# A three-stage kernel on one core: the halves of z take the way through device memory, four transfers home instead of sixteen

## The chip, the core and the metric

The kernel runs on one core of a Trainium2 chip. A core has five engines that run side by side, each through its own instruction stream in program order: TensorE (PE, matmuls; PEld is its weight load), VectorE (DVE), ScalarE (ACT), GpSimd (POOL), and SyncE (SP), which issues the transfers (DMAs) here. Matmuls write to PSUM, everything else works in SBUF; the inputs and the output are in device memory. An engine waits for another by semaphores.

The metric is the time of one execution on the device in microseconds (us). Before the change it is 1769.05 us, the median of 3 runs (1768.02 to 1769.48).

## The reference

Three stages, all in float32. First, attention in two steps through 32 packed tokens per head; then a mixture of 8 experts, each a two-layer network whose result is scaled by a balanced gate P; last, a two-layer network with a squared relu.

```python
p_packed = sm_attn(p, k, v)               # 4 batches, 8 heads, 576 tokens, 64 wide
out = sm_attn(q, p_packed, p_packed)
x = ...                                   # out as [2304, 512]
for e in range(8):                        # P: 8 rounds of row and column scaling
    h = np.maximum(x @ w1[e], 0.0)        # 512 -> 1024
    ye = h @ w2[e]                        # 1024 -> 512
    out += P[:, e:e + 1] * ye
h = x @ w_in                              # 512 -> 2048
g = s * (np.maximum(h, 0.0) ** 2) + b
return g @ w_out
```

## The kernel before

Every float32 operand of a large matmul is split in a high and a low part, and a product is three passes: high x high, high x low, low x high (PASSES). Tokens are kept transposed: xa holds the attention result as weights over the packed tokens of each batch, not x itself. So for the experts x @ w1 becomes two products: z = packed tokens @ w1, a small one, and then the attention weights times z. z is what the change is about.

The work of the experts is cut into 32 **units** u, 4 to an expert, each 256 columns of w1. Units 4 to 31 run in the function slotw, one call for each of the 4 batches, here called **blocks 0 to 3** of a unit. A block has five **places** n = 0 to 4. At each place stand, in this order: one of the four jobs j1 to j4 of mm1w (the first layer for this batch, matmuls of L524 into the PSUM tiles ps_a, ps_b and ps_e, followed by ACT's relu and DVE's low part into h); one tile2 of the block before (the second layer, 6 matmuls of L593 over 128 tokens, whose sum DVE puts into acc); and the side jobs given for this place. The four jobs use a form of matrix product with seven products for eight, hence the copies snap (L540) and sums (L487). Blocks 1 and 3 have four tile2 to run, blocks 0 and 2 have five. Within this stretch the order of each engine is the order written in the code (manual_schedule).

What the unit after this one needs is made by side jobs:

- w1_split (block 0): the high and low part of its w1 slice, into w1s.
- z_heads (block 2, places 0 and 2): z for one half of the heads, as 12 matmuls of L459, and two copies of ACT (L467) into a tile "stage". Partitions of stage are 32 packed tokens for each of 4 batches.
- z_home (same places): z has to lie by head group on the partitions, with the batches along the row. For each half 8 transfers of 64 KB go from stage to zp within SBUF (L476).
- z_add (L487, POOL): four sums and differences for one batch of z, from zp into sums.
- z_split (L494 and L495): for one batch, two casts on ACT give the high part zz, from zp and from sums, and two subtractions on POOL the low part. The matmuls of j1 of that batch's block read zz.

For batches 1 to 3, z_split stands at place 0 of the block before; z_add stands at place 3 two blocks before for batches 2 and 3, and at place 4 of block 3 of the unit before for batch 1. For batch 0 of the next unit z_add stands at place 1 of block 3 and z_split at place 3, after j4; the next block is block 0 of that next unit. The loads of w1 (place 2 of block 3) and of w2 (place 1 of block 0) follow z_home on SP, in the order of the code.

The tiles come from pools with few buffers: raw (2: w2 as loaded, one half of stage, and from unit 9 on also weights for the last stage), w1 (2, one of which holds the packed tokens for good), z (3: zp and two zz). A tile is written when the last reader of the one before in its buffer is through.

Of the kernel before, what the change touches and what calls it, by code (L numbers as in the profile page):

```python
# [9 lines left out]
F32 = mybir.dt.float32  # L10
# [6 lines left out]
B, H, S, HD, NPK = 4, 8, 576, 64, 32  # L17
# [3 lines left out]
NC = D // 128  # L21
FU = 256
# [21 lines left out]
def tile_kernel(ctx: ExitStack, tc: tile.TileContext, qT, kT, vv, pb, w1c, w2c, wcat64, wg, sv, bv, out):  # L44
    nc = tc.nc
    pool = lambda name, bufs=1, **k: ctx.enter_context(tc.tile_pool(name=name, bufs=bufs, **k))
    const = pool("const")
    big = pool("big")
    raw_p = pool("raw", 2)
    w_p = pool("w", 4)  # L50
    z_p = pool("z", 3)
    banks = {}

    def share(stack, **counts):
# [22 lines left out]
    def psa(tag, name):  # L77
        return banks[tag].tile([128, 512], F32, tag=tag, name=name)
# [32 lines left out]
    w1_p = []  # L111
# [12 lines left out]
    def load_w2(u, eng=G):  # L124
        r = raw_p.tile([128, 1024], F32, tag="raw", name="raw")
        nc.sync.dma_start(out=r, in_=w2c[u])
        yield
        w = w_new((2, u))
        if eng is V:
            V.tensor_copy(w[:, 0, :], r)  # L130
        else:
            A.copy(w[:, 0, :], r)
        eng.tensor_tensor(out=w[:, 1, :], in0=r, in1=w[:, 0, :].bitcast(F32), op=ALU.subtract)
# [286 lines left out]
    zq_, xt, wt_p, zplain = {}, [], [], []  # L420

    def zp_new():
        zplain[:] = [z_p.tile([128, B, 4, 128], F32, tag="z", name="zp")]
# [10 lines left out]
    pph, w1s, staged = [], {}, {}  # L434
# [16 lines left out]
    def z_heads(u, half):  # L451

        ps = [psa("y", "ps_z") for _ in range(2)]
        for j in range(2):
            c = 2 * half + j
            for n, (k, a) in enumerate(PASSES):
                for r in range(2):
                    rows = slice(64 * r, 64 * r + 64)
                    mmul(ps[r][:, j * FU:(j + 1) * FU], pph[0][rows, k, c, :], w1s[u][rows, a, c, :],  # L459
                         start=n == 0, stop=n == 2)  # L460
        if half:
            s_ = w1_p[-1].tile([128, 2, 2, FU], F32, tag="w1", name="stage1")
        else:
            s_ = raw_p.tile([128, 2, 2, FU], F32, tag="raw", name="stage0")
        staged[half] = s_
        for r in range(2):
            A.copy(s_[:, :, r, :], ps[r].rearrange("p (j m) -> p j m", j=2))  # L467

    def z_home(u, half):

        if half == 0:
            zp_new()
        for b in range(B):
            for j in range(2):
                c = 2 * half + j
                nc.sync.dma_start(out=zplain[0][32 * c:32 * c + 32, b].rearrange("k n m -> k (n m)"),  # L476
                                  in_=staged[half][32 * b:32 * b + 32, j].rearrange("k r m -> k (r m)"))

    z_sums = {}

# [211 lines left out]
    def slot1(u, pr, q, side=()):  # L692
        first = [lambda f=f: mm1a(u, pr, q, f) for f in range(UF)]
        coming.extend(made(u, pr, q))
        if u < UP:
            first.append(lambda: keep(u, q))
        slot(first, side, 0 if u < UP and (u, q) != (0, 2) else 1)

    def slotw(u, b, side):

        todo, jobs = ready[:], mm1w(u, b)
        ready[:] = made(u, b // 2, 2 * (b % 2)) + made(u, b // 2, 2 * (b % 2) + 1)
        for n in range(5):
            for q_ in (jobs, todo):
                if q_:
                    q_.pop(0)()
            for s in side.get(n, ()):
                s()
# [8 lines left out]
    def zjobs(u):  # L717

        ps = []
        t0, t1 = ("ym", "mm") if "m" in banks else ("yy", "yy")  # L720
        return [lambda: ps.extend((zmm(u, 0, tags=t0), zmm(u, 1, tags=t1))), lambda: zput(u, 0, ps[0]),
                lambda: zput(u, 1, ps[1])]
# [5 lines left out]
    def side1(u, pr, q):  # L728
        jobs = []
        if u + 1 < U1 and (pr, q) == (1, 0) and u + 1 != W0:  # L730
            jobs += zjobs(u + 1)
        if (pr, q) == (1, 1) and u + 2 < U1:
            jobs.append(lambda: load_w1(u + 2))
        if (pr, q) == (0, 1) and u + 1 < U1:
            jobs.append(lambda: list(load_w2(u + 1)))
        if u == W0 - 2 and pr == 1 and q % 2:
            jobs.append(lambda: behind_seam(x_add, q // 2))
        return jobs
# [8 lines left out]
    with tc.tile_pool(name="ppf", bufs=1) as ppf_p, tc.tile_pool(name="w1p", bufs=2) as w1_, ExitStack() as whole, ExitStack() as start:  # L747
# [3 lines left out]
        with tc.manual_schedule(), tc.tile_pool(name="at", bufs=1) as at_p, ExitStack() as early:  # L751
# [114 lines left out]
            for s in range(1, B - 1):  # L866
                n, last = s + 1, s == B - 2
# [19 lines left out]
        with tc.tile_pool(name="mid", bufs=1) as mid:  # L887
            share(start, y=3, h=2, m=3)
            bal = balance(mid)
            for u, pr, q in order[:cut]:  # L890
                side = []
                if u >= UP:
                    side = side1(u, pr, q)
                elif u == UP - 1:
                    side = zjobs(UP) if q == 2 else []
                elif q == 2:
                    side = [lambda: list(load_w2(UP))]
# [29 lines left out]
        with tc.manual_schedule():  # L927
            first = {(0, 1): [(w2_, W0), (x_split, 0)],
                     (0, 2): [(x_split, 1), (x_add, 2)],
                     (0, 3): [(w2_, W0)],  # L930
                     (1, 0): [(z_half, W0, 0), (z_half, W0, 1), (x_split, 2)],
                     (1, 1): [(x_add, 3), (load_w1, W0 + 1)],
                     (1, 2): [(z_add, W0, 0)],
                     (1, 3): [(z_split, W0, 0), (x_split, 3), (z_add, W0, 1)]}
            for u, pr, q in order[cut:]:
                slot1(u, pr, q, [lambda f=f, a=a: f(*a) for f, *a in first[pr, q]])
            for u in range(W0, U1):
                for b in range(B):
                    side, last = {n: [] for n in range(5)}, u == U1 - 1
                    if b + 1 < B:  # L940
                        side[0].append((z_split, u, b + 1))
                    if b + 2 < B:
                        side[3].append((z_add, u, b + 2))
                    if u == W0 and b == 0:
                        side[0].append((pp_split, ))
                    if last and b < 2:
                        side[2].append((split_plain, b, 0))
                        side[4].append((split_plain, b, 1))
                    if not last:
                        if b == 0:  # L950
                            side[1].append((w2_, u + 1))
                            side[2].append((w1_split, u + 1, 0))
                            side[4].append((w1_split, u + 1, 1))
                        if b == 1:
                            side[1].append((w2_, u + 1))
                        if b == 2:
                            side[0] += [(z_heads, u + 1, 0), (z_home, u + 1, 0)]
                            side[2] += [(z_heads, u + 1, 1), (z_home, u + 1, 1)]
                        if b == 3:
                            side[1].append((z_add, u + 1, 0))  # L960
                            side[3].append((z_split, u + 1, 0))
                            side[4].append((z_add, u + 1, 1))
                            if u + 2 < U1:
                                side[2].append((load_w1, u + 2))
                    if conv.get("at", 0) < steps and u > U1 // 4 or last and b:
                        side[(2, 0, 2, 1)[b]].append((more, ))
                    if last and b > 1:
                        for c in range(NC):
                            side[1 + c].append((flip, b - 2, c))
                    slotw(u, b, {n: [lambda f=f, a=a: f(*a) for f, *a in fs] for n, fs in side.items()})  # L970
        for v in range(U2):
            for b in range(NB):
                side = []
# [50 lines left out]
```

## Time and profile before

| | us |
|---|---|
| median of 3 runs | 1769.05 (1768.02 to 1769.48) |
| the profiled execution | 1768.22 |
| its span, from the first instruction to the last | 1766.4 |
| PE matmuls busy | 1703.8 (96%) |
| PE weight loads busy | 1453.1 (82%) |
| DVE busy | 1179.2 (67%) |
| POOL busy | 802.6 (45%) |
| ACT busy | 752.4 (43%) |

Units 4 to 31 fill the stretch from about 226 to 1350 us; before it stand attention, the gate and units 0 to 3, after it the last stage. The granted clock of PE was 0.999 of full speed over the span. A matmul's end is modelled in the records, and matmuls are pipelined, so the starts of groups tell more than their busy time. Busy shares of the other engines are low, but each works in order: what counts is whether a result is there when PE comes to it.

### The profile page before, as it was taken

How to read it: one execution, taken by the hardware profiler on the slowest of the kernel's cores; microseconds unless marked ns; L12 is line 12 of the kernel's file. 1: busy time of each engine (PE TensorE's matmuls, PEld its weight loads, DVE VectorE, ACT ScalarE, POOL GpSimd, SP SyncE). 2: the span in 40 equal slices, each digit the busy share in tenths (PEclk: the TensorE clock that was granted, in tenths of full speed). 3: DMA queues.
4: the chain of work that ended last, by engine and by line, in shares of the span. 5: the costliest groups of instructions: out<-in, count | busy, mean ns of one | idle time of the engine just before them, and what ended most of it. 6: DMA issues, size and time to landing. Idle time of an engine off the chain costs nothing.

```text
span 1766.4 us, 27541 instructions
## 1 busy us (share of the span) xinstructions
PE 1703.8 (96%) x10111; PEld 1453.1 (82%) x10111; DVE 1179.2 (67%) x2402; ACT 752.4 (43%) x1724; POOL 802.6 (45%) x970
## 2 busy tenths in 40 slices
PE   6999999999999999999999999999999999999999
PEld 4678877888888888788888888878888899999998
DVE  4646555566666666666666666656668888888864
ACT  3542265444444444444444444444444432322221
POOL 0322555555555454555555545455552233433332
PEclk9999999999999999999999999999999999999999
DMA  9510012212212222211221222221110111111102
GB/s 267 152 38 24 1 31 64 51 48 60 49 48 53 70 56 62 73 49 48 49 61 48 54 57 57 63 58 48 49 49 13 36 49 49 48 37 40 45 1 107
DMA packets 58135, 99.85 MB, mean 57 GB/s; under 512 B 10128, under 2 KB 31632, under 8 KB 58000
## 3 DMA queue, kind: packets, MB, share of 16 engines
q1 hardware_dynamic: 58000, 98.10, 20.6%
q8 instruction: 79, 1.29, 0.3%
q14 instruction: 56, 0.46, 0.1%
HBM read 65.03 MB, written 4.72 MB: 39 GB/s over the span
## 4 chain that ended last, share of the span: by engine, by line
PE 79%; DVE 7%; DMA 4%; SPq 3%; ACT 3%; POOL 2%; issue 2%; ACTq 0%; DVEq 0%
PE ps L593 46%; PE ps L620 10%; PE ps_a L524 9%; PE ps_e L524 4%; SPq L476 3%; PE ps_z L459 3%; PE ps L579 3%; PE ps_b L524 2%; POOL zz L495 2%; DMA zp<-stage 1%; DVE h L532 1%; DVE acc L608 1%; ACT zz L494 1%; DMA q__114<-qT 1%; ACT h L531 1%
## 5 line engine op out<-in xcount | busy, mean ns | idle before, releaser
L593 PE MATMUL ps<-w,h 128*128 128x512 f32 x4296 | 1085.1, 394 | 3.9 <-DVE xa L650 1.6
L593 PEld LDWEIGHTS ps<-w,h 128*128 128x128 f32 x4296 | 777.3, 188 | 145.1 <-issue 2.6
L608 DVE SCALAR_TENSOR_TENSOR acc<-ps,pm,acc 128x512 f32<-128x512 f32 x504 | 371.8, 744 | 164.0 <-PE ps L593 158.3
L540 ACT COPY snap<-ps_a 128x288 f32<-128x288 f32 x336 | 134.7, 401 | 249.8 <-PE ps_a L524 249.2
L495 POOL TENSOR_TENSOR zz<-zp,zz 128x384 fp32r<-128x384 f32 x112 | 113.5, 1013 | 258.8 <-ACT zz L494 258.8
L487 POOL TENSOR_TENSOR sums<-zp 128x128 f32<-128x128 f32 x224 | 104.3, 466 | 204.9 <-DMA zp<-stage 202.8
L630 POOL TENSOR_TENSOR h<-rg,h 128x384 fp32r<-128x384 f32 x96 | 103.0, 1073 | 201.1 <-ACT h L629 182.8
L524 PE MATMUL ps_a<-xa,zz 128*128 128x288 f32 x672 | 138.4, 308 | 37.2 <-ACT zz L494 18.9
L532 DVE SCALAR_TENSOR_TENSOR h<-ps_b,h 128x288 fp32r<-128x288 f32 x224 | 102.5, 458 | 106.4 <-ACT h L531 106.4
L524 PEld LDWEIGHTS ps_a<-xa,zz 128*128 128x128 f32 x672 | 110.3, 188 | 72.1 <-ACT zz L494 30.8
L531 ACT ACTIVATE h<-ps_b 128x288 fp32r<-128x288 f32 x224 | 92.1, 411 | 137.0 <-DVE ps_b L543 137.0
L620 PE MATMUL ps<-xa,w 128*128 128x384 f32 x576 | 147.2, 336 | 0.0
L620 PE MATMUL ps<-xt,w 128*128 128x384 f32 x576 | 147.0, 336 | 0.0
L495 POOL TENSOR_TENSOR zz<-sums,zz 128x512 fp32r<-128x512 f32 x112 | 146.4, 1307 | 0.0
L524 PE MATMUL ps_a<-xt,zz 128*128 128x288 f32 x672 | 128.9, 300 | 1.3 <-ACT snap L540 1.2
L524 PEld LDWEIGHTS ps_a<-xt,zz 128*128 128x128 f32 x672 | 111.6, 189 | 22.1 <-ACT snap L540 2.2
L524 PE MATMUL ps_e<-xt,zz 128*128 128x288 f32 x672 | 126.0, 296 | 0.0
L629 ACT CAST h<-rg 128x384 fp32r<-128x384 f32 x96 | 49.3, 514 | 174.8 <-DVE rg L628 174.7
L620 PEld LDWEIGHTS ps<-xa,w 128*128 128x128 f32 x576 | 104.9, 188 | 3.7
L620 PEld LDWEIGHTS ps<-xt,w 128*128 128x128 f32 x576 | 104.5, 188 | 0.0
L531 ACT ACTIVATE h<-ps_e 128x288 fp32r<-128x288 f32 x112 | 46.1, 411 | 131.7 <-DVE ps_e L543 131.7
L524 PEld LDWEIGHTS ps_e<-xt,zz 128*128 128x128 f32 x672 | 102.1, 189 | 0.1
(219 smaller groups left out, 2112.4 us busy)
## 6 DMA issues: line engine op xcount, KB each, us to landing
zp<-stage SPq DMA_DIRECT2D x432, 64.0 KB, 2.0
raw<-w2c SPq DMA_DIRECT2D x32, 512.0 KB, 4.9
raw<-wcat SPq DMA_DIRECT2D x32, 512.0 KB, 3.9
acc<-kT SPq DMA_DIRECT2D x8, 576.0 KB, 8.7
out<-acc SPq DMA_DIRECT2D x18, 256.0 KB, 2.0
acc<-vv SPq DMA_DIRECT2D x5, 576.0 KB, 10.2
q__112<-qT SPq DMA_DIRECT2D x1, 576.0 KB, 10.8
q__114<-qT SPq DMA_DIRECT2D x1, 576.0 KB, 13.3
```

Source lines behind the costliest of these rows:

```text
L459: mmul(ps[r][:, j * FU:(j + 1) * FU], pph[0][rows, k, c, :], w1s[u][rows, a, c, :], start=n == 0, stop=n == 2)
L476: nc.sync.dma_start(out=zplain[0][32 * c:32 * c + 32, b].rearrange("k n m -> k (n m)"), in_=staged[half][32 * b:32 * b + 32, j].rearrange( ...
L487: G.tensor_tensor(out=sums[:, n], in0=x_, in1=y_, op=op)
L495: G.tensor_tensor(out=zz[:, 1, o], in0=s_, in1=zz[:, 0, o].bitcast(F32), op=ALU.subtract)
L524: mmul(p_[:, :HB], zq_[u, b][:, a, LEFT[n], :], x_, start=start and m == 0, stop=m == 2, skip_group_check=True)
L531: A.activation(out=hh, in_=s_, func=AF.Relu)
L532: V.scalar_tensor_tensor(out=hl, in0=s_, scalar=0.0, in1=hh.bitcast(F32), op0=ALU.max, op1=ALU.subtract)
L540: A.copy(s_[n], p["a"][:, :HB])
L593: mmul(y, h[:, f, a, hc:hc + 128], ws[f][k], start=(n == 0), stop=(n == 3 * UF - 1))
L608: V.scalar_tensor_tensor(out=a, in0=y, scalar=pm[:, T, u // UE:u // UE + 1], in1=a, op0=ALU.mult, op1=ALU.add)
L620: mmul(p, w[:, a, c * 128:(c + 1) * 128], x_get(k, c, b), start=(n == 0), stop=(n == 3 * NC - 1))
L630: G.tensor_tensor(out=hl, in0=g, in1=hh.bitcast(F32), op=ALU.subtract)
```

## The change

The two halves of z are made a block sooner: z_heads stands at places 2 and 4 of block 1. Each half of stage, 128 partitions of 4 KB, goes out to device memory in one transfer of 512 KB, into a new pool "far" of 4 buffers there. z_home, once, at place 0 of block 2, brings z into zp in four transfers of 256 KB, one for each group of heads with all four batches. The halves of stage have swapped pools. For batch 0 of the next unit, z_add and z_split stand one place sooner in block 3: at places 0 and 2.

```diff
+    far_p = pool("far", 4, space=bass.MemoryType.DRAM)
...
         if half:
-            s_ = w1_p[-1].tile([128, 2, 2, FU], F32, tag="w1", name="stage1")
+            s_ = raw_p.tile([128, 2, 2, FU], F32, tag="raw", name="stage1")
         else:
-            s_ = raw_p.tile([128, 2, 2, FU], F32, tag="raw", name="stage0")
-        staged[half] = s_
+            s_ = w1_p[-1].tile([128, 2, 2, FU], F32, tag="w1", name="stage0")
         for r in range(2):
             A.copy(s_[:, :, r, :], ps[r].rearrange("p (j m) -> p j m", j=2))
-
-    def z_home(u, half):
-
-        if half == 0:
-            zp_new()
-        for b in range(B):
-            for j in range(2):
-                c = 2 * half + j
-                nc.sync.dma_start(out=zplain[0][32 * c:32 * c + 32, b].rearrange("k n m -> k (n m)"),
-                                  in_=staged[half][32 * b:32 * b + 32, j].rearrange("k r m -> k (r m)"))
+        staged[half] = far_p.tile([128, 2, 2 * FU], F32, tag="far", name="far")
+        nc.sync.dma_start(out=staged[half], in_=s_.rearrange("p j r m -> p j (r m)"))
+
+    def z_home(u):
+
+        zp_new()
+        for c in range(NC):
+            nc.sync.dma_start(out=zplain[0][32 * c:32 * c + 32].rearrange("k b n m -> k b (n m)"),
+                              in_=staged[c // 2][:, c % 2].rearrange("(b k) m -> k b m", b=B))
...
                         if b == 1:
                             side[1].append((w2_, u + 1))
+                            side[2].append((z_heads, u + 1, 0))
+                            side[4].append((z_heads, u + 1, 1))
                         if b == 2:
-                            side[0] += [(z_heads, u + 1, 0), (z_home, u + 1, 0)]
-                            side[2] += [(z_heads, u + 1, 1), (z_home, u + 1, 1)]
+                            side[0].append((z_home, u + 1))
                         if b == 3:
-                            side[1].append((z_add, u + 1, 0))
-                            side[3].append((z_split, u + 1, 0))
+                            side[0].append((z_add, u + 1, 0))
+                            side[2].append((z_split, u + 1, 0))
                             side[4].append((z_add, u + 1, 1))
```

On ACT, blocks 2 and 3 of a unit read so before, from block 2's job j2 to the first job of the next unit (stage_5359 is the second half of stage, zz<-zp and zz<-sums are z_split):

```order
L540 COPY snap<-ps_a 128x288 x2
L531 ACTIVATE h<-ps_b 128x288
L467 COPY stage_5359<-ps_z 128x2x256 x2
L531 ACTIVATE h<-ps_a 128x288
L531 ACTIVATE h<-ps_e 128x288
L540 COPY snap<-ps_a 128x288
L531 ACTIVATE h<-ps_b 128x288
L540 COPY snap<-ps_a 128x288 x2
L531 ACTIVATE h<-ps_b 128x288
L531 ACTIVATE h<-ps_a 128x288
L531 ACTIVATE h<-ps_e 128x288
L494 CAST zz<-zp 128x384
```

And so now, from the end of block 3's first job to the first job of the next unit (lines have moved by one):

```order
L539 COPY snap<-ps_a 128x288 x2
L530 ACTIVATE h<-ps_b 128x288
L493 CAST zz<-zp 128x384
L493 CAST zz<-sums 128x512
L530 ACTIVATE h<-ps_a 128x288
L530 ACTIVATE h<-ps_e 128x288
L539 COPY snap<-ps_a 128x288
```

z_split's casts have moved from behind j4's two relus (of ps_a and ps_e) to ahead of them.

In block 1 ACT now has the copies of both halves (stage_5204, stage_5247), the second pair ahead of the first snap of block 2:

```order
L467 COPY stage_5204<-ps_z 128x2x256 x2
L530 ACTIVATE h<-ps_a 128x288
L530 ACTIVATE h<-ps_e 128x288
L467 COPY stage_5247<-ps_z 128x2x256 x2
L539 COPY snap<-ps_a 128x288
```

The first pair stands ahead of j4's relus, as the second pair did in block 2 before.

On SP one unit's transfers read so before:

```order
L476 DMA zp<-stage_5300 32x512 x8
L476 DMA zp<-stage_5359 32x512 x8
L122 DMA w__5459<-w1c 64x4x256 x2
L126 DMA raw<-w2c 128x1024
```

And so now:

```order
L469 DMA far<-stage_5204 128x1024
L469 DMA far<-stage_5247 128x1024
L475 DMA zp<-far 32x4x512 x4
L123 DMA w__5410<-w1c 64x4x256 x2
L127 DMA raw<-w2c 128x1024
```

Six transfers stand where sixteen stood, with the same loads behind them.

## Rows read from the trace of the kernel before

**Rows 1.** Busy us (share of the span) and instructions of each engine.

```profile
PE 1703.8 (96%) x10111; PEld 1453.1 (82%) x10111; DVE 1179.2 (67%) x2402; ACT 752.4 (43%) x1724; POOL 802.6 (45%) x970
```

**Rows 2.** Waits of PE: total us, times, longest us.

```profile
PE ps_a L524 <- ACT zz L494: 18.9, 27, 1.5
PE ps_a L524 <- POOL zz L495: 18.3, 27, 0.7
```

**Rows 3.** Timeline of PE, one unit: start us, us, instructions [idle before <-releaser].

```profile
485.24 1.55 PE L593 MATMUL ps<-w,h 128*128 128x512 f32 x6
...
487.02 0.56 PE L524 MATMUL ps_b<-xa,zz 128*128 128x288 f32 x3
487.42 1.53 PE L593 MATMUL ps<-w,h 128*128 128x512 f32 x6
...
489.79 0.66 PE L524 MATMUL ps_a<-xt,zz 128*128 128x288 f32 x3
...
498.86 0.56 PE L524 MATMUL ps_b<-xa,zz 128*128 128x288 f32 x3
...
505.40 1.56 PE L593 MATMUL ps<-w,h 128*128 128x512 f32 x6
507.70 0.40 PE L524 MATMUL ps_a<-xa,zz 128*128 128x288 f32 x1 [0.75 <-ACT zz L494]
...
509.15 0.56 PE L524 MATMUL ps_b<-xa,zz 128*128 128x288 f32 x3
```

**Rows 4.** Timeline of PE, the first and the last of the 27 hand-overs.

```profile
262.84 1.56 PE L593 MATMUL ps<-w,h 128*128 128x512 f32 x6
...
267.33 0.56 PE L524 MATMUL ps_b<-xa,zz 128*128 128x288 f32 x3
...
1306.73 1.56 PE L593 MATMUL ps<-w,h 128*128 128x512 f32 x6
...
1310.38 0.56 PE L524 MATMUL ps_b<-xa,zz 128*128 128x288 f32 x3
```

**Rows 5.** Timeline of ACT, blocks 2 and 3 of the same unit.

```profile
494.94 1.07 ACT L467 COPY stage<-ps_z 128x512 f32<-128x512 f32 x2 [0.88 <-PE ps_z L459]
...
504.51 0.41 ACT L531 ACTIVATE h<-ps_b 128x288 fp32r<-128x288 f32 x1 [0.64 <-DVE ps_b L543]
505.20 0.41 ACT L531 ACTIVATE h<-ps_a 128x288 fp32r<-128x288 f32 x1 [0.28 <-PE ps_a L524]
506.84 0.41 ACT L531 ACTIVATE h<-ps_e 128x288 fp32r<-128x288 f32 x1 [1.23 <-DVE ps_e L543]
507.15 0.50 ACT L494 CAST zz<-zp 128x384 fp32r<-128x384 f32 x1
507.55 0.62 ACT L494 CAST zz<-sums 128x512 fp32r<-128x512 f32 x1
```

**Rows 6.** Timeline of DVE, end of block 3.

```profile
505.99 0.45 DVE L532 SCALAR_TENSOR_TENSOR h<-ps_a,h 128x288 fp32r<-128x288 f32 x1
506.35 0.46 DVE L543 TENSOR_TENSOR ps_e<-ps_e,snap 128x288 f32<-128x288 f32 x1
507.29 0.46 DVE L532 SCALAR_TENSOR_TENSOR h<-ps_e,h 128x288 fp32r<-128x288 f32 x1 [0.48 <-ACT h L531]
```

**Rows 7.** Timeline of POOL, blocks 2 and 3.

```profile
489.43 1.01 POOL L495 TENSOR_TENSOR zz<-zp,zz 128x384 fp32r<-128x384 f32 x1 [1.51 <-ACT zz L494]
...
498.86 0.46 POOL L487 TENSOR_TENSOR sums<-zp 128x128 f32<-128x128 f32 x1 [7.16 <-DMA zp<-stage]
```

**Rows 8.** Timeline of PE's weight loads, the first tile2 of block 2.

```profile
487.29 1.24 PEld L593 LDWEIGHTS ps<-w,h 128*128 128x128 f32 x6
```

**Rows 9.** Timeline of SP, block 2: start us, us of issuing, count.

```profile
491.04 10.07 SPq L476 DMA_DIRECT2D zp<-stage  x16
```

**Rows 10.** Transfers by line: count, KB each, median us from issue to landing.

```profile
raw<-w2c SPq DMA_DIRECT2D x32, 512.0 KB, 4.9
out<-acc SPq DMA_DIRECT2D x18, 256.0 KB, 2.0
```

## The prediction

> **What bounds the kernel now.** I read the busy table first: TensorE (PE) has matmuls for 1703.8 of 1766.4 us [rows 1], so only its gaps can be won back. The list of PE's waits comes next: two entries stand far above the rest, both at the matmuls of L524 into ps_a: 18.9 us over 27 times for ScalarE's (ACT's) cast into zz and 18.3 us over 27 times for GpSimd's (POOL's) low half of zz [rows 2]. 27 is the number of hand-overs from a unit u (a slice of an expert, 4 to 30 here) to u + 1. The timeline of one unit shows where they sit. At the end of block 1 the last tile2 starts at 485.24 and the first ps_b matmul at 487.02, 1.78 us later; at the end of block 3 the same two starts are 505.40 and 509.15, 3.75 us, with a 0.75 us wait for ACT inside [rows 3]. So this end costs 1.97 us more than a clean one. I read the same pair of starts at all 27 ends: 4.49 us at the first (262.84 to 267.33), 3.75 at 8, and 3.64 or 3.65 at the other 18, the last of them 1306.73 to 1310.38 [rows 4]. Less 1.78 each: 2.71 + 8 x 1.97 + 18 x 1.87 = **52.1 us**. That is the most that this change can win at this place.
>
> The two entries sum to only 37.2 us of idle [rows 2], since the idle is counted from a modelled end of a pipelined matmul; starts do not have that fault, so I take 52.1. The Trainium skill (Perfetto Trace Analysis, Identifying the Most-Contended Engine) says the same of matmul busy time, that it is a bad measure because matmuls are pipelined; by the idle alone the sum below would win 35, by the starts 50, and the trace here agrees with the rule.
>
> Why does PE wait there? ACT takes its work in program order. z_split's casts for the first quarter of u + 1 stand behind all of block 3's job j4, whose last relu into h starts at 506.84; the casts follow at 507.15 and 507.55 [rows 5], and PE, done with its last tile, needs their result at once. The data was no longer the cause: POOL's first subtraction, which waits for the transfers into zp, ran at 498.86 [rows 7], 8.3 us before the first cast. The wait is one of order; the order is what the late transfers had required.
>
> **The change part by part.**
>
> *z_split a place earlier (block 3, place 2 instead of 3).* The casts now stand between j3's relu (504.51) and j4's relu of ps_a. On ACT an operation starts 0.10 us before its forerunner ends (506.84 + 0.41 against 507.15) [rows 5], so the casts run at 504.82 and 505.22, and POOL's first low half (1.01 us [rows 7]) is done by about 506.4. A clean end would start ps_a's matmuls near 506.8. High and low halves are both there: the two waits go, **-52.1 us**.
>
> What is late next? The casts push j4's relu of ps_a from 505.20 to 505.74, ending at 506.15. On VectorE (DVE) the subtraction behind it started at 505.99 and now starts at 506.19: DVE was itself late there, so only 0.20 of the 0.54 us goes on. The sum into ps_e (506.35) and ACT's relu of it (506.84) shift by 0.20 and the relu ends at 507.45; DVE's low half (507.29, 0.46) ends at 507.95 [rows 5, 6]. The first tile2 of the next block needs both: its weight load stands 2.05 us behind the last tile's start in the clean end (485.24 to 487.29 [rows 3, 8]), hence at 507.45 here. The high half is a dead heat; the low half, wanted by the third load (1.24 us for six [rows 8], so 0.42 later, 507.87), is 0.08 late. I take **+0.08 x 27 = +2.2 us**; the bounds are 0 and, if the 0.92 us that ACT spends on the casts (504.82 to 505.74) went on whole, 0.9 us an end.
>
> *z_heads a block sooner (block 1, places 2 and 4, instead of block 2, places 0 and 2).* The matmuls are the same. One call makes the start of a tile and that of the next L524 group 2.37 us apart (487.42 to 489.79 [rows 3]) where a tile alone takes 1.4, so 1.0 us, and it goes along: 0 us net. The two ACT copies (1.07 us [rows 5]) of the second call now stand ahead of block 2's first snap; it ends some 1.5 us after that block's first matmul, and the next matmuls into ps_a come 2.2 us after it (two groups of 0.4, 487.02 to 487.42, and a tile of 1.4 [rows 3]). Hidden. Without that cover it would be at most the copies' 1.07 x 27 = 29 us, which I give little weight. The first call's copies delay j4's relus as its copies did in block 2, and here a second z_heads of 1.0 us follows before the next block wants h.
>
> *The transfers.* Sixteen issues took 10.07 us of SyncE's queue (SP), 0.63 each, from 491.04 [rows 9]. Now two of 512 KB go out in block 1 and four of 256 KB come home in block 2. No row shows a write to device memory of 512 KB; the nearest are 256 KB in 2.0 us (out<-acc) and a 512 KB read in 4.9 us that stood behind other reads [rows 10]; I take 2.0 to 4.9 for each leg. Count from block 2's first ps_b start (487.02 before). The second half's copies end at about +0.8, its way out is issued by +1.4 and lands at +3.4 to +6.3. zp is free when POOL has read it: 489.43 + 1.01, +3.4 [rows 7]. Four issues of 0.63, the third not ahead of the second half's landing: the last is issued at +5.9 to +7.6 and lands at +7.9 to +12.5. Block 3's first ps_b start, now without two z_heads, is at +11.84 - 2.0 = +9.8 (487.02 to 498.86 [rows 3]); call it T. So z is home at T - 1.9 to T + 2.7. POOL's four subtractions take 4 x 0.46 = 1.84 us [rows 7], and the second cast wants them at 505.22, T + 6.4: z is wanted by T + 4.5. Slack 1.8 to 6.4 us: **0 us**. Behind the homes on SP stand the loads of w1 and w2; they now leave some 4 us sooner and are wanted a block later: 0. No other wait is on the path.
>
> *Sum.* The profiled execution took 1768.2 us (span 1766.4 and 1.8 around it), 0.8 under the median of 1769.05. 1768.2 - 52.1 + 2.2 = 1718.3; against the median, **1719 us**.
>
> **The rivals.**
>
> *Rival 1: the casts hold j4 up in full.* For it: ACT is in order, and the next block's first tile needs the relu of ps_e. Against it: 0.34 of the 0.54 us falls into DVE's own lateness [rows 5, 6]. If instead the first tile waits 0.9 us, and a stop costs 0.27 more than its idle (1.43 of idle for 1.97, in two stops), that is 1.2 x 27 = 32 us of the 52: 1769 - 20 = 1749. Same if the snap of block 2 loses its cover.
>
> *Rival 2, slower: the way through device memory is late.* One mechanism: two legs in sequence for the second half, and z_add now wants all four transfers, not a quarter of each. Its place is the second cast of block 3; ACT stands there, and j4's relus and the next block with it. It begins to cost when z lands after T + 4.5, and decides when it lands after T + 6.5, 3.8 us past my late end. If each leg took one and a half times the longest row, 7.4 us, the second half would be out at +8.8, the last home issued at +10.1 and landed at +17.5, T + 7.7: 3.2 us late, 1.2 more than the wait of today, 27 x 1.2 = 32: 1801. Against it: it needs legs of 7.4 us where the longest of the two rows has 4.9, and that one for a load that stood behind others. The Trainium skill (DMA: Bandwidth & Descriptors, Anatomy of one DMA) warns that the completion of a write can take "a surprisingly long" time "especially when the write target is HBM"; the one row of such a write, 2.0 us, does not show it, and no run here shows one of 512 KB.
>
> *Rival 3: nothing changes*, since the wait only gets another name (POOL's low half late for another reason). POOL has nothing else in that stretch of block 3, so this has little for it: 1769.
>
> **How the numbers follow.** Forecast 0.77, rival 1 0.12, rival 2 0.08, rival 3 0.03. What a measurement can tell here is about 0.2%, 3.5 us; forecast and rival 1 are both beyond it. Faster 0.89, same 0.03, slower 0.08. Low end 1713: the residue at 0 and the small waits for snap gone too. High end 1746: it takes in most of the way to rival 1. Outside lie rivals 2 and 3 and half of rival 1, less than 2 in 10 with a little below.
>
> **What would show it.** In the changed profile PE's two waits at ps_a for zz fall from 27 each to nearly none, the pair of starts at block 3's end is 1.8 to 1.9, a unit takes about 38.2 us and not 40.1, and a new small wait of L593 for h may show. POOL's first subtraction of block 3 waits for zp<-far until at most T + 2.7. If ACT's casts wait for POOL's sums, or if the pair of starts stays above 2.5, I am wrong; if a third wait of 1 us or more shows elsewhere in the unit, my covers in block 1 or 2 failed.

## The result: faster by 2.9%, as forecast

The changed kernel takes **1717.02 us** (median of 6 runs, 1714.77 to 1718.88) where the kernel before took 1767.84 in the runs beside it: a ratio of 0.9712 (95% interval 0.9699 to 0.9724), 50.8 us less. The forecast was 1719, and the forecast's case is the one that came.

The profiled execution took 1714.77 us, with a span of 1713.0. The busy table of its page answers to [rows 1]:

```profile
PE 1689.0 (99%) x10111; PEld 1452.1 (85%) x10111; DVE 1181.4 (69%) x2402; ACT 744.2 (43%) x1724; POOL 804.5 (47%) x970
```

PE, DVE, ACT and POOL have the same number of instructions as before; what went is waiting. PE's busy time fell as well, though its matmuls are the same. Over the stretch from unit 4's first ps_b matmul to the last block's (us; busy us and count of PE, PEld, DVE, ACT, POOL; granted clock, DMA share, GB/s), before and now:

```profile
225.65:1339.40 1113.75, 1074.21 (x5981) 908.49 (x5980) 704.77 (x1336) 532.22 (x1215) 587.12 (x753) 1.00 0.21 54
224.04:1285.70 1061.66, 1059.35 (x5982) 906.88 (x5980) 707.96 (x1336) 523.89 (x1215) 588.98 (x753) 1.00 0.31 83
```

37.2 us of idle and 14.9 us of what is booked as busy make up the 52.1 us by which it is shorter: a part of the stops had been booked as busy time. The list of PE's waits (total us, times, longest) answers to [rows 2]:

```profile
PE ps_s L241 <- DMA acc<-kT: 5.7, 2, 5.3
PE ps_s L241 <- DVE z L418: 2.3, 1, 2.3
PE ps_t L276 <- ACT a L260: 1.8, 1, 1.8
```

Both waits for zz, 37.2 us, have left the list. What heads it now is the first loads, before any unit. The timeline of PE at a hand-over, the end of block 3 and the start of the next unit, answers to [rows 3]:

```profile
484.02 0.56 PE L523 MATMUL ps_b<-xa,zz 128*128 128x288 f32 x3
...
490.55 1.56 PE L592 MATMUL ps<-w,h 128*128 128x512 f32 x6
491.95 0.56 PE L523 MATMUL ps_a<-xa,zz 128*128 128x288 f32 x3
492.34 0.56 PE L523 MATMUL ps_b<-xa,zz 128*128 128x288 f32 x3
492.73 1.64 PE L592 MATMUL ps<-w,h 128*128 128x512 f32 x6
494.21 0.56 PE L523 MATMUL ps_a<-xt,zz 128*128 128x288 f32 x3
```

From the last tile's start to the first ps_b matmul it is now 1.79 us (490.55 to 492.34), not 3.75: a clean end. 484.02 is T here, block 3's first ps_b start. One thing is left: the first tile2 after it takes 1.48 us to the next group (492.73 to 494.21), 0.1 more than its like. ACT, DVE and the weight loads (PEld) say why (timelines, answering to [rows 5, 6, 8]):

```profile
489.67 0.41 ACT L530 ACTIVATE h<-ps_b 128x288 fp32r<-128x288 f32 x1 [0.64 <-DVE ps_b L542]
489.98 0.50 ACT L493 CAST zz<-zp 128x384 fp32r<-128x384 f32 x1
490.38 0.62 ACT L493 CAST zz<-sums 128x512 fp32r<-128x512 f32 x1
490.90 0.41 ACT L530 ACTIVATE h<-ps_a 128x288 fp32r<-128x288 f32 x1
492.21 0.41 ACT L530 ACTIVATE h<-ps_e 128x288 fp32r<-128x288 f32 x1 [0.90 <-DVE ps_e L542]
```

```profile
491.34 0.46 DVE L531 SCALAR_TENSOR_TENSOR h<-ps_a,h 128x288 fp32r<-128x288 f32 x1
491.72 0.46 DVE L542 TENSOR_TENSOR ps_e<-ps_e,snap 128x288 f32<-128x288 f32 x1
492.65 0.46 DVE L531 SCALAR_TENSOR_TENSOR h<-ps_e,h 128x288 fp32r<-128x288 f32 x1 [0.48 <-ACT h L530]
```

```profile
492.67 0.30 PEld L592 LDWEIGHTS ps<-w,h 128*128 128x128 f32 x2
493.16 0.77 PEld L592 LDWEIGHTS ps<-w,h 128*128 128x128 f32 x4 [0.19 <-DVE h L531]
```

The casts stand between j3's relu and j4's two, and the third weight load of the next tile waits 0.19 us for DVE's low half of h. POOL's first subtraction, which says when z is home, and SP's issues (answering to [rows 7, 9]) and the transfers by line (to [rows 10]; median from issue to landing):

```profile
485.11 0.46 POOL L486 TENSOR_TENSOR sums<-zp 128x128 f32<-128x128 f32 x1 [6.07 <-DMA zp<-far]
```

```profile
471.83 3.57 SPq L469 DMA_DIRECT2D far<-stage  x2
477.82 1.74 SPq L475 DMA_DIRECT2D zp<-far  x4
479.61 1.20 SPq L123 DMA_DIRECT2D w__5410<-w1c  x2
```

```profile
far<-stage SPq DMA_DIRECT2D x54, 512.0 KB, 2.6
zp<-far SPq DMA_DIRECT2D x108, 256.0 KB, 4.9
raw<-w2c SPq DMA_DIRECT2D x32, 512.0 KB, 7.6
```

z is home at T + 1.1 here. Over the 27 hand-overs POOL starts at T + 1.17 in the mean, where the sixteen transfers let it start at T + 0.38: by device memory z comes 0.8 us later, though it leaves a block sooner.

### The profile page after: what moved, and what is told of

It is laid out like the page before. It is cut to its first block, busy times and chain, and to the rows that moved or that the text cites. A ratio compares the mean times of both kernels' runs of the same rounds, so it can differ in the third digit from the quotient of the medians.

```text
span 1713.0 us, 27134 instructions
## 1 busy us (share of the span) xinstructions
PE 1689.0 (99%) x10111; PEld 1452.1 (85%) x10111; DVE 1181.4 (69%) x2402; ACT 744.2 (43%) x1724; POOL 804.5 (47%) x970
## 4 chain that ended last, share of the span: by engine, by line
PE 93%; DVE 5%; ACT 1%; POOL 1%; issue 0%; DMA 0%; SPq 0%; ACTq 0%; DVEq 0%
PE ps L592 56%; PE ps_a L523 11%; PE ps L619 10%; PE ps_e L523 5%; PE ps_z L460 3%; PE ps L578 3%; PE ps_b L523 3%; PE ps_z L407 1%; PE ps_t L276 0%; PE ps_v L286 0%; DVE raw L175 0%; DVE ex L167 0%; DVE ex L164 0%; DMA acc<-kT 0%; PE ps_q L301 0%
## 5 line engine op out<-in xcount | busy, mean ns | idle before, releaser
L523 PE MATMUL ps_a<-xa,zz 128*128 128x288 f32 x672 | 131.4, 304 | 0.0
```

The source lines that it names most:

```text
L523: mmul(p_[:, :HB], zq_[u, b][:, a, LEFT[n], :], x_, start=start and m == 0, stop=m == 2, skip_group_check=True)
```

## Experiments

The question after the result is which half of the change won the time: the order in block 3, or the way of z. Theory: the order alone; the way of z and the earlier z_heads win and cost nothing. The rival: they were needed, since the order had been written for late transfers.

**The order alone (e1).** The kernel before, with one line moved:

```diff
                             side[1].append((z_add, u + 1, 0))
-                            side[3].append((z_split, u + 1, 0))
+                            side[2].append((z_split, u + 1, 0))
```

> The kernel before with one edit: z_split of the next unit's first batch stands at place 2 of block 3 and not at place 3; sixteen transfers within SBUF, z_heads in block 2, z_add at place 1. Theory (the wait was one of order on ACT; the transfers were not late): z was home when POOL first subtracted, 498.86, and its sums are done at 500.7, 4 us ahead of the place where the casts now stand. The two waits go as in the changed kernel: a gain of 48 to 53 us, 0.970 to 0.973 of before. Rival (the way through device memory and the earlier z_heads are needed for it): the casts now wait for z or push other work, and less than 25 us is won, 0.985 or more.

Measured: 1718.03 us, 0.9712 of before (0.9699 to 0.9726), the very ratio of the whole change. Both waits for zz are gone from the list of PE's waits, a unit takes 38.25 us in the mean (38.25 in the changed kernel, 40.17 before), and POOL starts at T + 0.36, as before. The last tile and the first ps_b matmul at a hand-over of e1, and the head of its list of PE's waits:

```profile
493.53 1.56 PE L593 MATMUL ps<-w,h 128*128 128x512 f32 x6
494.93 0.55 PE L524 MATMUL ps_a<-xa,zz 128*128 128x288 f32 x3
495.32 0.56 PE L524 MATMUL ps_b<-xa,zz 128*128 128x288 f32 x3
```

```profile
PE ps_s L240 <- DMA acc<-kT: 6.3, 2, 5.4
```

It is a clean end of 1.79 us. The one moved line is the whole gain.

**The way through device memory alone (e2).** The changed kernel with z_add and z_split back at places 1 and 3:

```diff
-                            side[0].append((z_add, u + 1, 0))
-                            side[2].append((z_split, u + 1, 0))
+                            side[1].append((z_add, u + 1, 0))
+                            side[3].append((z_split, u + 1, 0))
```

> The changed kernel with z_add and z_split of the next unit's first batch back at places 1 and 3 of block 3: six transfers by device memory, z_heads in block 1. Theory (order): PE waits for zz as before, 1.3 to 1.5 us a unit; 0.998 to 1.002 of before, a unit of 40.0 to 40.2 us. Rival (the transfers won the time): 0.975 to 0.99.

Measured: 1768.49 us, 0.9997 (0.9988 to 1.0006). PE's waits are back to the tenth of a microsecond:

```profile
PE ps_a L523 <- ACT zz L493: 18.9, 27, 1.5
PE ps_a L523 <- POOL zz L494: 18.3, 27, 0.7
```

So the new transfers, the earlier z_heads and the copies ahead of block 2's snap cost nothing either, as the prediction had it. Here the casts want z later than in the changed kernel; that the way of z costs nothing at the new place too is seen in the changed kernel and e1, which have the same ratio to the kernel before.

**How late z may come (e5, e6).** The changed kernel with 2 or 6 idle transfers ahead of the four home (here 6):

```diff
         zp_new()
+        for _ in range(6):
+            nc.sync.dma_start(out=far_p.tile([128, 1024], F32, tag="idle", bufs=2, name="idle"), in_=w2c[u])
         for c in range(NC):
```

> The changed kernel with two idle transfers of 512 KB (w2c of the unit into a spare place in device memory) ahead of the four that bring z home. Theory: z_add has slack; in the changed kernel POOL's first subtraction starts 1.1 us after block 3's first ps_b matmul (T) and the second cast wants its sums at T + 6.4, so the first subtraction may start up to T + 4.5. Two idle transfers put it at T + 2 to T + 5: no more than 0.5 us a unit is lost, 0.970 to 0.980 of before. Rival (no slack: each us that z comes later is lost): 1 to 4 us a unit, 27 to 108 us over the changed kernel.

Measured with two: 1717.81 us, 0.9716 (0.97 to 0.9732). POOL starts at T + 3.42 in the mean (2.8 to 4.6), 2.2 us later than in the changed kernel, and nothing is lost that the times could show (a unit takes 38.27 us in the mean, 38.25 in the changed kernel): the slack is real. At the latest start, T + 4.6, the second cast comes 0.2 us late, as a slack to T + 4.5 has it. Two units took 38.53 us: in the block 3 ahead of them POOL's sums, now later, ran beside an operation of DVE that took 0.69 us and not 0.41, a collision that e3 shows below.

> The changed kernel with six idle transfers of 512 KB ahead of the four that bring z home. Theory: once the first subtraction starts past T + 4.5 (T: block 3's first ps_b matmul), ACT stands at the second cast, j4's relus behind it, and PE loses what it is past that, one for one: with the first subtraction at T + 5 to T + 10, 0.5 to 5.5 us a unit, 14 to 150 us over the changed kernel; the trace's own start of that subtraction gives the loss within 0.5 us a unit. Rival (PE has other work to run ahead with, or DVE hides it): less than half of that.

Measured with six: 1917.53 us, 1.0844 (1.0827 to 1.086), 200 us over the changed kernel. POOL starts at T + 10.41 in the mean, 5.9 past T + 4.5; the next first ps_b comes at T + 13.84 and not T + 8.33, 5.5 us later. That far it is nearly one for one. But a unit takes 45.43 us, 7.2 more, and not within the 0.5 us that the expectation allowed. The other 1.7 us lie behind the hand-over, 1.1 of them in the first tile (2.54 us in the mean, 1.42 in the changed kernel). One hand-over, in PE's timeline and then in a table of stretches (columns as in the result):

```profile
762.76 1.56 PE L594 MATMUL ps<-w,h 128*128 128x512 f32 x6
766.96 0.61 PE L525 MATMUL ps_a<-xa,zz 128*128 128x288 f32 x1 [2.63 <-ACT zz L495]
769.27 0.85 PE L525 MATMUL ps_a<-xa,zz 128*128 128x288 f32 x2 [1.71 <-POOL zz L496]
769.91 0.92 PE L525 MATMUL ps_b<-xa,zz 128*128 128x288 f32 x3
770.63 2.88 PE L594 MATMUL ps<-w,h 128*128 128x512 f32 x6
773.31 0.63 PE L525 MATMUL ps_a<-xt,zz 128*128 128x288 f32 x3
```

```profile
764.00:765.00 1.00, 0.32 (x2) 0.00 (x0) 0.00 (x0) 0.00 (x0) 0.00 (x0) 1.00 1.08 202
766.50:767.00 0.50, 0.04 (x1) 0.05 (x1) 0.00 (x0) 0.40 (x1) 0.42 (x2) 0.62 1.17 211
767.00:768.00 1.00, 0.56 (x1) 0.24 (x1) 0.00 (x0) 0.00 (x0) 1.00 (x3) 0.50 1.19 253
772.00:773.00 1.00, 1.00 (x4) 0.78 (x3) 0.51 (x2) 0.92 (x3) 0.38 (x2) 0.50 0.00 0
774.00:775.00 1.00, 1.00 (x7) 0.87 (x6) 0.30 (x1) 0.38 (x1) 1.00 (x1) 1.00 0.00 0
```

At the end of the first stop the granted clock falls from 1.00 to 0.50, its lower level (1.2 GHz), and it is back at 1.00 in the stretch from 774; the first tile, in between, takes 2.68 us (770.63 to 773.31) where it takes 1.38 at the upper level. The wait itself was priced nearly rightly; what the expectation left out is the lower clock of the work behind a stop of this length.

**The casts' price on ACT (e7).** Each of the two casts done twice for a unit's first batch:

```diff
         for o, s_ in z_sums[u, b]:
-            A.copy(zz[:, 0, o], s_)
+            for _ in range(2 if b == 0 else 1):
+                A.copy(zz[:, 0, o], s_)
```

> The changed kernel with each of the two casts for a unit's first batch done twice, so that ACT has 0.92 us more between j3's and j4's relus in block 3. Theory: DVE's own lateness had hidden 0.34 us of the first 0.54; nothing is left to hide, so j4's relu of ps_a, the sum into ps_e and the relu of ps_e shift by 0.92 us, and the next unit's first tile2 waits 1.0 us for h: 25 to 35 us over the changed kernel, 0.985 to 0.991 of before. Rival (the casts are hidden whole, the 0.1 us a unit comes from elsewhere): within 5 us of the changed kernel.

Measured: 1749.58 us, 0.9896 (0.9881 to 0.991), 32.6 us over the changed kernel and inside 25 to 35. The wait is where it was expected, at the first tile, for a relu into h; 27 of the 28 times are the hand-overs. By the starts the first tile comes 0.94 us later there (1.33 us behind the first ps_b matmul, 0.39 in the changed kernel), where 1.0 was expected:

```profile
PE ps L593 <- ACT h L531: 21.6, 28, 0.8
```

So one pair of casts is nearly hidden and the second is paid in full, 1.16 us a unit for 0.92 of ACT: that is rival 1's mechanism, which the changed kernel just escapes.

**One place sooner still (e3, e4).** z_split at place 1, on the changed kernel and, with z_add at place 0, on the kernel before:

```diff
-                            side[2].append((z_split, u + 1, 0))
+                            side[1].append((z_split, u + 1, 0))
```

> The changed kernel with z_split of the next unit's first batch one place sooner again, at place 1 of block 3. Theory: the low half of h that the next unit's first tile2 waits for is late by 0.1 us a unit because the casts stand ahead of j4's relu; at place 1 they stand ahead of j3's snap, where ACT is idle for 1.8 us, so this residue goes: 2 to 3 us below the changed kernel, 0.969 to 0.970 of before where the changed kernel has 0.971. The second cast then waits for POOL's sums by 0.2 us at most. Rival (the 0.1 us is not from the casts): the same as the changed kernel, within 1 us; or the casts wait for POOL and hold up j3, 5 us or more above it.

> The kernel before with z_add of the next unit's first batch at place 0 and z_split at place 1 of block 3, transfers as before. Theory: z is home at about block 3's first ps_b matmul, the sums are done 1.9 us after it, and ACT comes to the casts some 2.8 us after it: no wait for z, and the residue of 0.1 us a unit goes too: 0.968 to 0.971 of before, 1 to 4 us below the kernel that only moves z_split to place 2. Rival: sixteen transfers are too late for this place, ACT waits for sums by 0.5 us or more and j3 with it, and it is slower than the kernel that moves z_split to place 2 by 5 us or more.

Measured: 1722.45 us, 0.9742 (0.9729 to 0.9756), and 1719.96 us, 0.9724 (0.9711 to 0.9737). Neither won anything: e4 cannot be told from e1, e3 is 5 us above the changed kernel, and the reason is none of those that I had written. ACT's waits do not reach PE: in e3 the first cast starts at T + 2.7; the second waits for POOL's sums in a few hand-overs, 0.6 us at most; and behind the first hand-over ACT is free each time before j3's snap is due. But 12 hand-overs have an operation of DVE's unpacking of the last stage's weights in block 3, and from the third unit on the units around them take up to 38.66 us in e3 and 38.62 in e4, those without it 38.18 and 38.16. DVE and POOL in e3, in one of the longer ones:

```profile
491.74 0.99 DVE L175 SCALAR_TENSOR_TENSOR w_plain<-raw,ex 128x256 f32<-128x256 f32 x1
492.66 0.45 DVE L542 TENSOR_TENSOR ps_b<-ps_e,snap 128x288 f32<-128x288 f32 x1
```

```profile
490.18 1.02 POOL L494 TENSOR_TENSOR zz<-zp,zz 128x384 fp32r<-128x384 f32 x1 [0.40 <-ACT zz L493]
491.14 1.30 POOL L494 TENSOR_TENSOR zz<-sums,zz 128x512 fp32r<-128x512 f32 x1
```

The DVE operation takes 0.99 us; in the changed kernel all 8 of its kind in this stretch take 0.41 to 0.42 (minimum, median and maximum in ns, first and last start in us):

```profile
L175 DVE SCALAR_TENSOR_TENSOR w_plain<-raw,ex x8: 414/416/417, 488.8 to 1016.5; 128x256 f32<-128x256 f32 x8
```

It starts while POOL is in an operation that ends at 492.44, and ends 0.29 us after that. The sum behind it is late by 0.6 us, then j3's relu, then h. The earlier casts had set POOL on top of it.

**The collision taken away (e8, e9).** To e3 and e4 one more edit, which puts that DVE operation where no POOL operation runs beside it:

```diff
-                        side[(2, 0, 2, 1)[b]].append((more, ))
+                        side[(2, 0, 2, 4)[b]].append((more, ))
```

> The kernel with z_split at place 1 (e3) with one more edit: in block 3 DVE's step of unpacking the last stage's weights (one operation of 128x256) stands at place 4 and not at place 1. Theory for e3's miss: at place 1 the casts let POOL's low parts of zz run from T + 3.3 to T + 5.6 (T: block 3's first ps_b matmul), on top of that DVE operation, which then takes 0.99 us instead of 0.41 (0.85 instead of 0.28 for another form) and makes j3's sum and the relus behind it 0.6 us late. With the operation moved to where POOL is idle, no unit takes more than 38.3 us, those operations take 0.28 and 0.41 again, and the time is 1715 to 1717.5, 0.970 to 0.9715 of before; 5 us below e3. Rival (the casts ahead of j3's snap cost the time themselves): units of 38.6 us remain and the time is within 1.5 us of e3's 1722.

> The kernel before with z_add at place 0 and z_split at place 1 of block 3 (e4) and the same DVE operation at place 4: no transfer by way of device memory. Theory: as e8, 1715 to 1717.5, no unit over 38.3 us, 3 us below e4; equal to the changed kernel within what can be told. Rival (collision is not what e4 had): units of 38.6 us remain, 1719 to 1721.

Measured: 1715.54 us, 0.9699 (0.9686 to 0.9712), and 1716.56 us, 0.9703 (0.969 to 0.9716). After the first two units, every unit takes 38.18 us in e8, and 38.16 to 38.21 in e9. The DVE operations in e8:

```profile
L175 DVE SCALAR_TENSOR_TENSOR w_plain<-raw,ex x8: 411/416/418, 497.0 to 1019.5; 128x256 f32<-128x256 f32 x8
```

The longest takes 418 ns, where e3 has up to 989. e8 is 6.9 us below e3, and the intervals of their ratios lie apart: the collision was the cause. e9 is 3.4 us below e4; those intervals overlap, but the long units are gone there too. The two are 1.5 and 0.5 us below the changed kernel, and again the intervals overlap, so no version here is shown to beat it; e9 equals it without device memory.

## Why the prediction was right, point by point

*The hand-over, -52.1 us.* Right in place, cause and size. The 27 pairs of starts sum to 100.1 us before and to 48.3 now, 51.8 less; all ends are clean but the first, which takes 1.95 us. The whole stretch from unit 4's first ps_b matmul to the last block's went from 1113.75 to 1061.66 us, also 52.1 less, but that is a sum of three: the 51.8, the residue below, and about 1 us won in the first units, which the prediction did not count. 0.6 of it lies in the first tile behind the first hand-over: before, the stops there were the longest (1.49 and 0.67 us), the granted clock went down to 0.50 behind them, and that tile took 2.02 us. Reading starts and not the idle time decided the forecast: the idle sum of 37.2 us would have put the time at about 1734. Only the sentence that PE's gaps alone can be won back was too narrow: 14.9 us of its busy time went with them. The span shrank by 53.5; 1.6 us of that lies ahead of the units, whose start lay between 224.6 and 228.2 us in the other kernels too, so it is scatter.

*z_split a place earlier.* The chain that the prediction worked out came true to 0.01 us in the unit shown: casts at T + 5.96 and T + 6.36, the relu of ps_a at T + 6.88, of ps_e at T + 8.19 (8.18 foretold). DVE's own lateness hid 0.34 of 0.54 us, and e7 shows what is paid when nothing is left to hide.

*The residue, +2.2 us.* Right mechanism, too large: the first tile is 0.09 us longer at 8 of 27 hand-overs (1.46 to 1.48 us against 1.38 to 1.40) and 0.14 at the first, 0.8 us in all. I had charged 0.08 to all 27. The 8 are those of the 3.75 us ends, where ACT was 0.11 us later already before; the unit from which the prediction read its rows is one of them.

*z_heads a block sooner, 0 us.* Right: e2 carries it and is 0.9997 of before (0.9988 to 1.0006).

*The transfers, 0 us.* Right. z was foretold at T - 1.9 to T + 2.7 and starts POOL at T + 1.17 in the mean, T + 0.9 to T + 2.5. The leg out took 2.6 us, the leg home 4.9 at the median (6.0 at most), the bounds being 2.0 and 4.9; an issue took 0.33 to 0.44, not 0.63, and the loads behind left 8 us sooner, not 4 (479.61, T - 4.4, against 502.70, T + 3.8). The slack to T + 4.5 shows in e5, and e6 shows rival 2's mechanism: far beyond that the kernel is slower than before. z never came near that in the changed kernel. The page of the Trainium skill on DMA (DMA: Bandwidth & Descriptors, Anatomy of one DMA), cited beside rival 2, warns, of transfers that GpSimd issues, of slow completions in device memory; SyncE issues them here, and the 54 writes of 512 KB here landed in 2.6 us at the median and 3.9 at most, so this trace does not show one.

*One sentence was wrong:* "the order is what the late transfers had required". e1 has the sixteen transfers and the new order, and wins everything. The order could have been changed alone; z had been home in time all along.

## What to carry to other kernels

When PE waits for an operation of an engine that works in order, look at what stands ahead of that operation in program order, and at when its inputs were there: here they had been there 6 us, and one line was the gain. Take the loss from the starts of neighbouring groups, in a clean and in a stopped place, not from the idle column. Before moving an operation further forward, look at what its consumers on a third engine will then run beside.

## What the runs showed of the hardware

A DVE operation with both sources in SBUF took 0.99 us beside a POOL operation and 0.41 alone (e3), and ended 0.29 us after POOL's own. Its longer time is listed as busy time of DVE, not as a wait. DVE operations with one source in PSUM, as L542 at 492.66, kept their 0.45 beside POOL (PSUM is not PE's alone: ACT and DVE read it, and DVE writes it, as in this operation). The Trainium skill (SBUF — State Buffer, SBUF: two separate sides) describes this as a port pair that DVE and GpSimd hold in turn for a whole instruction, with two SBUF inputs on DVE's side against a GpSimd operation that reads SBUF; the trace agrees. An operation of the same unpacking with a single source in SBUF, L164, was held up as well, 0.85 us and not 0.28 in e3; the same section names DVE's two-port modes as another case, and no run here shows whether L164 is one.

When PE had stood for 2.6 us, the granted clock went down to 0.50; it was still there after a further stop of 1.7 us, and the first tile took twice its time (e6, 766.5 to 774 us). In the kernel before, two stops of 0.64 to 0.75 us left the first tile at 1.37 to 1.39 us at 26 hand-overs; at the first, with stops of 1.49 and 0.67 us, it took 2.02 us (267.73 to 269.75), and the granted clock of the stretch from 269 to 270 us was 0.50:

```profile
269.00:270.00 1.00, 1.00 (x5) 0.81 (x3) 0.42 (x1) 0.94 (x2) 1.00 (x3) 0.50 0.00 0
```
